# Decode attention and mixer on one core: loads by half chunks at the layer changes, and a sixth kept V chunk

## The chip, the cores and the metric

The kernel runs on one core of a Trainium2 chip. The metric is the device time of one execution in microseconds (us); the median of the runs is compared. In the profile PE is TensorE, DVE is VectorE, ACT is ScalarE, POOL is GpSimd and SP is the engine whose queue issues nearly all transfers here. The core has 16 DMA engines, and every transfer of this kernel is spread over all of them.

## What is computed

Two tokens (a batch of 2, one position each, 512 channels) pass through two layers. A layer is an attention block followed by a small mixer, each with a residual:

```
x = x + attention(layernorm(x), k_cache, v_cache, wq, wo)
x = x + mixer(layernorm(x), w1, b1, w2, b2)      # layernorm, one 1 x 1792 product, gelu, 1792 x 1
x = x + attention(layernorm(x), k_cache, v_cache, wq, wo)
x = x + mixer(layernorm(x), w1, b1, w2, b2)
```

The attention has 32 query heads on 8 heads of keys and values, with 32768 cached keys of 128 channels for each of the 2 x 8 pairs of token and head. All is float32. Both layers use the same caches and weights. K and V of one pair are 16.8 MB each, so one layer reads 537 MB and two layers 1074 MB, less what stays on the chip between them.

## The kernel before, in words

**Units and chunks.** A unit is (layer, token b, head h), and there are 32 of them, numbered n in an order of their own. K and V of a unit are cut into 8 chunks c of 4096 keys. One chunk fills 16 KB in each of the 128 partitions and weighs 2.1 MB ("2048 KB" in the profile). For a K chunk PE runs 8 products (line 359, shown as 16 matmul records, because each float32 product leaves two), for a V chunk 8 more (line 492). In most of the run, chunks are loaded four at a time in one transfer of 8 MB.

**Memory.** The tile `mem` holds 14 numbered cells of one chunk each (the last one shorter). Cells 0 to 8 are the ring for passing chunks, cells 9 to 12 hold the weights of the heads that pass, and cell 13 is a rest of 10 KB per partition. Around the changes of layer the cells 3 to 9, 11 and 13 are needed for what stays, and the passing chunks have cells 0, 1 and 2 alone: this is `limit=RING` with `RING` 3, and there each transfer is one chunk.

**What stays.** Head 7 is the keeper. Its units of layer 0 and layer 1 for the same token follow one another closely (units 13 and 15 for token 0, units 16 and 18 for token 1), so that what was loaded for layer 0 is read again for layer 1 without a second load. `KEPT_K` lists three K chunks (2, 4, 5 in cells 9, 7, 8); `KEPT` lists the V chunks with the number of quads (eighths of a chunk) and the cell: 1, 3, 5, 6, 7 whole, and of chunk 4 five quads. Two more quads of chunk 4 are set aside in PSUM (`IN_PSUM`).

**The two changes of layer.** Unit 13 is (0, 0, 7) and ends layer 0 for token 0; its mixer must be done before the layer-1 unit 15 = (1, 0, 7) can form its query. Between them unit 14 = (0, 1, 5) is worked on, and the mixer's steps are spread between its K chunks (lines 714 and 190). The same happens for token 1 with units 16 = (0, 1, 7), 17 = (1, 0, 5) and 18 = (1, 1, 7). Unit 19 is (1, 1, 5), and unit 20 = (1, 0, 0) is the first of layer 1 on a passing head, whose weights (2.1 MB of Wq and Wo) are loaded into cell 9 during unit 19's K chunks.

**The order of work.** The order is written out by a planner: `parts` gives the pieces in which a unit's K and V are loaded, `stream` sorts them, and `at(time, ...)` hangs the small steps to slots of that order (one slot is one chunk). The last loop walks through `stream`: it issues a load, then the products of that piece, then the steps due. PE executes this order. SP executes the loads in the same order, one after another, and runs ahead as far as memory allows: a load whose place is still being read waits on PE's semaphore, and every load behind it waits as well.

**Places.** `buffer` (line 126) takes the place in the ring that was touched longest ago. `load_k` and `load_v` (lines 336 and 424) issue the transfers at lines 344, 433 (a kept part) and 446. `load_weights` issues at line 115.

Of the kernel before, what the change touches and what calls it, by code (L numbers as in the profile page):

```python
# [13 lines left out]
P = 128  # L14
CK = 4096
JT = CK // P
NG = 4
SUB = 2
PACK = 4
GROUPS = ((0, 4), (4, 4))  # L20
RING = 3
# [1 line left out]


KEPT_K = {2: 9, 4: 7, 5: 8}
KEPT = {1: (8, 6), 3: (8, 11), 4: (5, 13), 5: (8, 3), 6: (8, 4), 7: (8, 5)}
REST = 5
IN_PSUM = (4, 5, 2)
ASIDE = 3
# [3 lines left out]
PIECES = (32, 16, 8, 4, 4)  # L33
THIN = 16
QT = 4
# [7 lines left out]
def gqa_mixer_kernel(ctx: ExitStack, tc: tile.TileContext, x, kt, v, wqo, cols, out):  # L43
# [17 lines left out]
    nc = tc.nc  # L61
    B, D = out.shape
    U = kt.shape[0]
    DH = D // NG
    NCH = kt.shape[1] // (CK * DH)
    HKV = U // B
# [31 lines left out]
    WCELL0, WCELLS = RING * RING, 4  # L98
# [3 lines left out]
    mem = const.tile([P, (WCELL0 + WCELLS) * CK + REST * QT * DH], F32, name="mem")  # L102

    def cells(k, m=1):
        return mem[:, k * CK : (k + m) * CK]
# [9 lines left out]
        nc.sync.dma_start(cells(cell), wqo[h])  # L115


    used = [0] * (WCELL0 + WCELLS + 1)
    clock = [0]

    def touch(k, m=1):
        clock[0] += 1
        for j in range(k, k + m):
            used[j] = clock[0]

    def buffer(m, limit):

        k = min(range(0, limit - m + 1, m if limit % m == 0 else RING), key=lambda k: max(used[k : k + m]))
        touch(k, m)
        return cells(k, m)  # L130

    load_weights(0, WCELL0)
    cols_sb = sm["cols"]
# [35 lines left out]
    kept = [pfix.tile([P, 512], F32, name=f"kept{k}") for k in range(IN_PSUM[2])]  # L169
# [29 lines left out]
    def first_input():  # L199

        t = spot()
        cen, sq = (t[:, k * B * DT : (k + 1) * B * DT].rearrange("p (b d) -> p b d", b=B) for k in range(2))
        m, rs = (t[:, (2 * DT + k) * B : (2 * DT + k + 1) * B] for k in range(2))
        p = misc()
        nc.tensor.matmul(p[:, : B * DT], ones, xcols.rearrange("p b d -> p (b d)"), start=True, stop=True)
        nc.vector.tensor_reduce(m, p[:, : B * DT].rearrange("p (b d) -> p b d", b=B), axis=AX.X, op=ALU.add)
        nc.vector.tensor_scalar_mul(m, m, 1.0 / D)
        for b in range(B):
            nc.vector.tensor_scalar_sub(cen[:, b, :], xcols[:, b, :], m[:, b : b + 1])
        nc.vector.tensor_mul(sq, cen, cen)  # L210
# [107 lines left out]
    BESIDE = N3 + 1, 5  # L318
# [11 lines left out]
    def piece(a, u, c, m):  # L330

        c0, size = next(g for g in GROUPS if g[0] <= c < sum(g))
        rows = a[u, c0 * CK * DH : (c0 + size) * CK * DH].rearrange("(p f) -> p f", p=P)
        return rows[:, (c - c0) * CK : (c - c0 + m) * CK]

    def load_k(n, c, m, limit):
        layer, b, h = unit_of(n)
        stay = h == keeper and c in KEPT_K
        own = KEPT_K[c] if stay else KEPT[1][1] if (n, c) == BESIDE else None
        if own is not None:  # L340
            touch(own, m)
        t = buffer(m, limit) if own is None else cells(own, m)
        if not (stay and layer):
            nc.sync.dma_start(t, piece(kt, b * HKV + h, c, m))
        for j in range(m):
            k_at[n, c + j] = t[:, j * CK : (j + 1) * CK]

    def k_chunk(n, c):

        kc = k_at.pop((n, c))  # L350
        half, i = divmod(c, PACK)
        if i == 0:
            sc_ps[n, half] = pscore.tile([P, 512], F32, name="scores")
        w = CK // (NG * SUB)
        for k in range(SUB):
            at = R * (SUB * i + k)
            q = qpad[n % 2][:, 28 - at : 60 - at]
            for g in range(NG):
                nc.tensor.matmul(  # L359
                    sc_ps[n, half][32 * g : 32 * g + 32, :],  # L360
                    q,
                    kc[:, (k * NG + g) * w : (k * NG + g + 1) * w],
                    start=(i == 0 and k == 0),
                    stop=(i == PACK - 1 and k == SUB - 1),
                )
        if i == PACK - 1:
            if half == 0:
                mx[n] = field(n, 0, HALVES)
            nc.vector.tensor_reduce(mx[n][:, half : half + 1], sc_ps[n, half], axis=AX.X, op=ALU.max)  # L369
# [49 lines left out]
    def stays(n, c):  # L419

        quads, cell = KEPT.get(c, (0, 0)) if unit_of(n)[2] == keeper else (0, 0)
        return quads, mem[:, cell * CK : cell * CK + quads * QT * DH]

    def load_v(n, c, m, limit):
        layer, b, h = unit_of(n)
        src = piece(v, b * HKV + h, c, m)
        stay, own = stays(n, c)
        if stay:
            touch(KEPT[c][1])
        w = QT * DH  # L430
        f = stay * w
        if stay and layer == 0:
            nc.sync.dma_start(own, src[:, :f])
        if stay == JT // QT:
            return
        t = buffer(m, limit)
        banks = []
        if stay and (c, stay) == IN_PSUM[:2]:
            banks = [(k, t[:, f + i * w : f + (i + 1) * w]) for i, k in enumerate(kept)]
        if layer:  # L440
            for k, quad in banks:
                nc.vector.tensor_copy(quad, k)
                f += w
        last = n == NU - 1 and c + m == NCH
        for k in PIECES if last else (m * JT - f // DH,):
            nc.sync.dma_start(t[:, f : f + k * DH], src[:, f : f + k * DH])
            f += k * DH
        if not layer:
            for k, quad in banks:
                nc.vector.tensor_copy(k, quad)  # L450
        for j in range(m):
            v_at[n, c + j] = t[:, j * CK : (j + 1) * CK]

    last_sums = {}

# [21 lines left out]
        nc.vector.tensor_mul(oT[n][:, :, 1], po[:, :R], rl[n])  # L477

    def v_chunk(n, c):
        w = QT * DH  # L480
        very_last = n == NU - 1 and c == NCH - 1
        stay, own = stays(n, c)
        vc = v_at.pop((n, c), None)
        half, i = divmod(c, PACK)


        a, c2 = divmod(i, PACK // 2)
        quads = JT // QT - (THIN // QT if very_last else 0)
        for q in range(quads):
            g = q % NG  # L490
            col = (c2 * (JT // QT) + q) * 32 + a * R * QT
            nc.tensor.matmul(  # L492
                acc[32 * g : 32 * g + R * QT, :],
                S[half][:, col : col + R * QT],
                (own if q < stay else vc)[:, q * w : (q + 1) * w],
                start=(c == 0 and q < NG),
                stop=(c == NCH - 1 and q >= quads - NG),
            )
        if very_last:
            add_tiles()  # L500

        for j in range(quads * QT, JT):
            q, t = divmod(j, QT)
            g = j % NG
            col = (c2 * (JT // QT) + q) * 32 + a * R * QT + t * R
            nc.tensor.matmul(
                kept[0][32 * g : 32 * g + R, :DH],
                S[half][:, col : col + R],
                vc[:, j * DH : (j + 1) * DH],
                start=(j < quads * QT + NG),  # L510
                stop=True,
                skip_group_check=True,
            )
# [107 lines left out]
    def last_mixer(n):  # L621
# [2 lines left out]
        layer, b, h = unit_of(n)  # L624
        w = D // 2
        st, mv, rs = ln_st.rearrange("p (k s) -> p k s", k=2), ln_mv, ln_rs
        space = buffer(2, 2 * RING)
        tiles = [space[:, k * D : (k + 1) * D] for k in range(JT2)]
        flat = tiles[JT2 - 1]
        y = row_tile()  # L630
# [152 lines left out]
    for n in range(NU):  # L783
# [55 lines left out]
        if units[n] == lay[layer, b][-1]:  # L839
# [30 lines left out]
            if layer + 1 < LAYERS:  # L870
                at(e + 2, to_columns, key)
                mixed[key] = e + 2

    first_input()
    for step in range(3):
        make_q(0, step)
# [4 lines left out]

    t = 0
    for _, is_v, n, c, m, limit in stream:
        if not is_v and (n, c) in SOONER:
            load_v(*SOONER[n, c], m, limit)
        if not is_v or (n, c) not in SOONER.values():
            (load_v if is_v else load_k)(n, c, m, limit)
        for j in range(m):
            (v_chunk if is_v else k_chunk)(n, c + j)
            t += 1  # L890
            run(t)
# [58 lines left out]
```

## Time and profile before

| | |
|---|---|
| median of 3 runs | 2502.08 us (2501.8 to 2502.96) |
| span of the profiled execution | 2500.0 us (the median of the runs lies 2.1 us above it) |
| PE busy | 1383.1 us, 55% of the span |
| DVE, ACT busy | 222.4 us and 185.4 us |
| moved by DMA | 1067.23 MB, mean 427 GB/s |
| read from HBM | 1065.91 MB |
| transfers of one chunk of K, of V | 44 and 35, 2048 KB each |
| transfers of four chunks | 48 of K and 47 of V |

The page shows in its first part how long each engine was busy, and in its second part the span in 40 slices with the busy tenths of each engine, the granted clock of PE and the DMA's rate. Its third part shows the DMA queues; q1 is SP's. The chain of waits goes back from the last instruction to what released it at each step. A timeline row has its start, its length, the engine, the line, the operation, the tiles and the number of records, and in brackets how long the engine stood idle before it and what ended that. On the chain a piece named DMA begins with the issue of the transfer and ends when the engine that waited for it could start.

### The profile page before, as it was taken

Reading aid. Unit: us, or ns where it says so; the run is one execution under the profiler, and the core shown is the slowest. Engines: PE = TensorE matmul, PEld = TensorE weight load, DVE = VectorE, ACT = ScalarE, POOL = GpSimd, SP = SyncE. Lnnn points to the kernel's source line nnn. Section 1 sums busy time; section 2 is a strip of 40 time slices with the busy share of each in tenths; the row PEclk is TensorE's granted clock in tenths of the full one; section 3 lists DMA queues with packets and bytes.
Section 4 is the critical chain, followed back from the end, with each engine's and each line's share of the span. In section 5 each row is a group of like instructions: output and inputs, shape, how many; then the busy total and the mean of one; then the engine's idle time right before and its main releaser. Section 6 shows DMA issues by size and latency. Waiting matters only on the chain.

```text
span 2500.0 us, 20528 instructions
## 1 busy us (share of the span) xinstructions
PE 1383.1 (55%) x9326; PEld 375.5 (15%) x9326; DVE 222.4 (9%) x610; ACT 185.4 (7%) x550; POOL 4.9 (0%) x17
## 2 busy tenths in 40 slices
PE   4545554645445554657667775455546454455546
PEld 1111111111111111111111211111111111111112
DVE  0000000000000000001111110000000000010002
ACT  0000000000000000001012010000000000011002
POOL 0000000000000000000000000000000000000000
PEclk8777777877777777879888977677778777777778
DMA  9999999999999999999999999999999999999996
GB/s 419 436 433 430 433 435 430 436 430 430 433 433 431 434 429 435 425 423 421 426 427 427 423 430 430 432 435 434 432 430 435 435 423 435 433 433 426 432 429 292
DMA packets 31200, 1067.23 MB, mean 427 GB/s; under 512 B 3717, under 2 KB 3721, under 8 KB 4618
## 3 DMA queue, kind: packets, MB, share of 16 engines
q1 hardware_dynamic: 30824, 1065.89, 99.2%
q8 instruction: 73, 1.20, 0.2%
q14 instruction: 13, 0.11, 0.0%
q10 hardware_dynamic: 290, 0.04, 0.0%
HBM read 1065.91 MB, written 0.00 MB: 426 GB/s over the span
## 4 chain that ended last, share of the span: by engine, by line
DMA 74%; PE 24%; issue 0%; DVE 0%; ACT 0%; SPq 0%; POOL 0%; ACTq 0%
DMA mem<-in_v_dram 65%; PE acc L492 19%; DMA mem<-in_kt_dram 9%; PE scores L359 3%; PE bcast L292 1%; PE rows L190 0%; PE small L385 0%; PE small L521 0%; ACT S L714 0%; PE kept L671 0%; PE small L379 0%; PE small L256 0%; ACT mem L681 0%; ACT mem L693 0%; PE bcast L575 0%
## 5 line engine op out<-in xcount | busy, mean ns | idle before, releaser
L359 PE MATMUL scores<-mem,small_sb 128*32 128x512 f32 x4096 | 620.6, 722 | 592.0 <-DMA mem<-in_kt_dram 591.6
L492 PE MATMUL acc<-mem,S 128*16 128x512 f32 x4088 | 614.1, 738 | 468.2 <-DMA mem<-in_v_dram 462.5
L359 PEld LDWEIGHTS scores<-mem,small_sb 128*32 128x32 f32 x4096 | 151.1, 127 | 970.5 <-issue 895.5
L396 ACT ACTIVATE S<-S,small_sb 128x128 f32<-128x128 f32 x240 | 123.5, 519 | 2102.4 <-DVE small_sb L387 1636.6
L492 PEld LDWEIGHTS acc<-mem,S 128*16 128x16 f32 x4088 | 134.8, 110 | 831.7 <-issue 693.2
L369 DVE TENSOR_REDUCE small_sb<-scores 128x1 f32<-128x512 f32 x64 | 44.2, 691 | 874.1 <-PE scores L359 874.1
L391 DVE STREAM_TRANSPOSE S<-scores 128x512 f32<-128x512 f32 x64 | 45.4, 710 | 131.4 <-PE acc L492 131.4
L292 PE MATMUL kept<-mem,small_sb 128*2 128x512 f32 x104 | 50.9, 615 | 1.7 <-DVE small_sb L218 1.7
L190 PE MATMUL rows<-mem,small_sb 128*1 128x512 f32 (+1 forms) x276 | 48.4, 603 | 3.1 <-ACT mem L714 2.4
L396 ACT ACTIVATION_READ_ACCUMULATOR S<-S,small_sb 128x1 f32 x240 | 44.8, 187 | 0.0
L381 DVE TENSOR_REDUCE small_sb<-small 1x4 f32<-1x128 f32 x32 | 8.8, 276 | 280.7 <-PE small L379 280.7
L460 DVE SCALAR_TENSOR_TENSOR S<-acc,small_sb,S 128x128 f32<-128x128 f32 x93 | 32.6, 351 | 3.3
L523 DVE RECIPROCAL small_sb<-small 128x4 f32<-128x4 f32 x32 | 5.9, 185 | 292.1 <-PE small L521 292.1
L531 DVE TENSOR_TENSOR small_sb<-small,small_sb 128x4 f32<-128x4 f32 x31 | 5.1, 164 | 278.2 <-PE small L529 278.2
L714 ACT ACTIVATE S<-bcast,small_sb 128x512 f32<-128x512 f32 x28 | 20.7, 775 | 96.1 <-DVE small_sb L583 82.6
L190 PE MATMUL rows<-S,small_sb 128*1 128x512 f32 (+1 forms) x56 | 21.2, 591 | 8.1 <-ACT S L714 8.1
L304 PE MATMUL small<-small_sb,mem 2*128 2x2 f32 x112 | 15.1, 252 | 17.9 <-DVE mem L301 17.9
L458 DVE TENSOR_SCALAR S<-acc,small_sb 128x128 f32<-128x128 f32 x31 | 10.8, 350 | 128.8 <-PE acc L492 128.8
L292 PE MATMUL bcast<-mem,small_sb 128*1 128x512 f32 (+1 forms) x40 | 19.1, 609 | 1.2 <-DVE small_sb L261 1.2
L529 PEld LDWEIGHTS small<-small_sb,S 128*128 128x128 f32 x62 | 11.6, 234 | 48.8 <-issue 36.0
L304 PEld LDWEIGHTS small<-small_sb,mem 2*128 2x128 f32 x112 | 13.9, 190 | 30.5 <-DVE mem L301 27.3
L529 PE MATMUL small<-small_sb,S 128*128 128x4 f32 x62 | 14.3, 301 | 4.9 <-DVE S L460 4.9
(132 smaller groups left out, 267.7 us busy)
## 6 DMA issues: line engine op xcount, KB each, us to landing
mem<-in_kt_dram SPq DMA_DIRECT2D x44, 2048.0 KB, 12.7
mem<-in_v_dram SPq DMA_DIRECT2D x35, 2048.0 KB, 13.9
mem<-in_v_dram SPq DMA_DIRECT2D x9, 4096.0 KB, 32.7
mem<-in_wqo_dram SPq DMA_DIRECT2D x14, 2048.0 KB, 33.8
mem<-in_kt_dram SPq DMA_DIRECT2D x7, 4096.0 KB, 25.7
mem<-in_v_dram SPq DMA_DIRECT2D x2, 1280.0 KB, 13.6
mem<-in_v_dram SPq DMA_DIRECT2D x2, 768.0 KB, 18.6
mem<-in_v_dram SPq DMA_DIRECT2D x4, 256.0 KB, 28.8
```

The lines of the kernel that those rows point to most:

```text
L190: nc.tensor.matmul(rows[32 * g : 32 * g + b + 1, :], weights if b else weights[:, 1:], row, start=False, stop=True, skip_group_check=True,)
L292: nc.tensor.matmul(q_ps[n][:m, :], xnT[:, d, b : b + m], wq_at(h)[:, d, :], start=(d == 0), stop=(d == DT - 1),)
L304: nc.tensor.matmul(pt[:, r * m : (r + 1) * m], q_row[n][:m, r * DH : (r + 1) * DH], ident[:m, :m], start=True, stop=True,)
L359: nc.tensor.matmul(sc_ps[n, half][32 * g : 32 * g + 32, :], q, kc[:, (k * NG + g) * w : (k * NG + g + 1) * w], start=(i == 0 and k == 0), ...
L369: nc.vector.tensor_reduce(mx[n][:, half : half + 1], sc_ps[n, half], axis=AX.X, op=ALU.max)
L391: nc.vector.transpose(S[half], sc_ps[n, half])
L396: nc.scalar.activation(s[:, :, h], s[:, :, h], AF.Exp, bias=neg[n][:, h : h + 1], scale=SCALE, accum_out=lsum[n][:, half, h : h + 1],)
L458: nc.vector.tensor_scalar_mul(t, acc[:, :DH], mask[:, 0:1])
L460: nc.vector.scalar_tensor_tensor(t, acc[:, k * DH : (k + 1) * DH], mask[:, k : k + 1], t, op0=ALU.mult, op1=ALU.add)
L492: nc.tensor.matmul(acc[32 * g : 32 * g + R * QT, :], S[half][:, col : col + R * QT], (own if q < stay else vc)[:, q * w : (q + 1) * w], st ...
L529: nc.tensor.matmul(po[:, :R], asb, selh, start=True, stop=True)
L714: nc.scalar.activation(hid[key, f], px[key], AF.Gelu_apprx_tanh, bias=shift[key][:, f : f + 1], scale=slope[key][:, f : f + 1],)
```

## The change

The loads at `limit == RING` no longer take the oldest of three whole cells. The bookkeeping in slots (`busy`, `now`, `booked`, `closed`) says until when each half cell is read, when a cell is booked for something that stays, and when it closes. `spread` looks for a whole cell among 0 to 9 that has been idle for two slots and stays clear until the chunk is done; if there is one, the chunk is loaded whole as before. If there is none, the chunk is loaded as two transfers of half a chunk, 8 KB per partition, each into the half cell that is free first. The products now read their quads from a list (`quads`), so that the two halves need not lie side by side; their number and order stay. `KEPT` gains chunk 2, all 8 quads, in cell 2, which leaves cells 0 and 1, four halves, in the tightest stretch.

```diff
-KEPT = {1: (8, 6), 3: (8, 11), 4: (5, 13), 5: (8, 3), 6: (8, 4), 7: (8, 5)}
+KEPT = {1: (8, 6), 2: (8, 2), 3: (8, 11), 4: (5, 13), 5: (8, 3), 6: (8, 4), 7: (8, 5)}
...
-    def buffer(m, limit):
-
-        k = min(range(0, limit - m + 1, m if limit % m == 0 else RING), key=lambda k: max(used[k : k + m]))
-        touch(k, m)
+    def buffer(m, limit, until):
+
+        k = min(range(0, limit - m + 1, m), key=lambda k: idle(k, m))
+        assert idle(k, m) <= now[0]
+        hold(k, m, until)
         return cells(k, m)
+
+    def half(until):
+
+        k = min((j for j in range(2 * NCH) if clear(j // 2, until)), key=lambda j: busy[j])
+        assert busy[k] <= now[0]
+        busy[k] = until
+        return mem[:, k * HB : (k + 1) * HB]
+
+    def clear(k, until):
+
+        return until <= closed.get(k, until) and all(r <= now[0] or r >= until + 1.5 for r in booked.get(k, ()))
+
+    def spread(until):
+
+        whole = [k for k in range(WCELL0 + 1) if idle(k) <= now[0] - 2 and clear(k, until)]
+        if whole:
+            k = min(whole, key=idle)
+            hold(k, 1, until)
+            return [cells(k)]
+        return [half(until - 0.5), half(until)]
...
-        t = buffer(m, limit) if own is None else cells(own, m)
-        if not (stay and layer):
-            nc.sync.dma_start(t, piece(kt, b * HKV + h, c, m))
+        until = k_done[n, c + m - 1]
...
+        elif limit == RING:
+            bufs = spread(until)
+        else:
+            bufs = [buffer(m, limit, until)]
+        src, f = piece(kt, b * HKV + h, c, m), 0
+        for t in bufs:
+            if not (stay and layer):
+                nc.sync.dma_start(t, src[:, f : f + t.shape[-1]])
+            f += t.shape[-1]
...
-                    kc[:, (k * NG + g) * w : (k * NG + g + 1) * w],
+                    kc[k * NG + g],
...
+    for n in (N1, N2):
+        for c in KEPT_K:
+            booked.setdefault(KEPT_K[c], []).append(k_done[n, c] - 1)
+        for c in KEPT:
+            first = next((k_done[k] - 1 for k, e in SOONER.items() if e == (n, c)), v_done[n, c] - 1)
+            booked.setdefault(KEPT[c][1], []).append(first)
+    booked[KEPT[1][1]].append(k_done[BESIDE] - 1)
+    closed[WCELL0], closed[WCELL0 - 1] = kbeg[N3 + 2] - 10, kbeg[N3 + 2] - 8
```

`load_v` is changed in the same way; the part of chunk 4 that doesn't stay goes into one half cell.

In the changed program the order of the products, of the steps on DVE and ACT, and of the chunks that are loaded stays as it was. SP's transfers of `mem` are these: at each of the two changes 11 chunks (K chunks 4 to 7 and V chunks 0 to 4 of unit 14, and K chunks 0 and 1 of unit 15; units 17 and 18 at the second change) come as 22 halves into cells 0 and 1, all others as whole chunks; V chunk 2 of units 15 and 18 isn't loaded. Later V chunk 6 of unit 14 and K chunk 7 of unit 15 go to cell 9, some chunks to cells 7 and 8. K chunk 3 of unit 19 goes to cell 9, and the next transfer in SP's order is the weights of unit 20's head, into cell 9 as well. Before, that K chunk went to cell 1.

More of the change, by code (lines that the diff above doesn't have):

```diff
@@ L115, in load_weights, with hold, idle, quads @@
         nc.sync.dma_start(cells(cell), wqo[h])
[L118 to L124, printed above, removed]
-    def buffer(m, limit):
-        k = min(range(0, limit - m + 1, m if limit % m == 0 else RING), key=lambda k: max(used[k : k + m]))
-        touch(k, m)
-        return cells(k, m)
+    HB = CK // 2
+    busy = [0] * 2 * (WCELL0 + WCELLS + 1)
+    now = [0]
+    def hold(k, m, until):
+        for j in range(2 * k, 2 * (k + m)):
+            busy[j] = max(busy[j], until - 0.5 * (m == 1 and j == 2 * k))
+    def idle(k, m=1):
+        return max(busy[2 * k : 2 * (k + m)])
+    def buffer(m, limit, until):
+        k = min(range(0, limit - m + 1, m), key=lambda k: idle(k, m))
+        assert idle(k, m) <= now[0]
+        hold(k, m, until)
+        return cells(k, m)
+    def half(until):
[12 more added lines that the diff above has]
+        return [half(until - 0.5), half(until)]
+    def quads(a):
+        w = QT * P
+        return [a[:, i : i + w] for i in range(0, a.shape[-1], w)]
+    booked, closed = {}, {}
     load_weights(0, WCELL0)
@@ L339, in load_k @@
         own = KEPT_K[c] if stay else KEPT[1][1] if (n, c) == BESIDE else None
+        until = k_done[n, c + m - 1]
         if own is not None:
-            touch(own, m)
-        t = buffer(m, limit) if own is None else cells(own, m)
-        if not (stay and layer):
-            nc.sync.dma_start(t, piece(kt, b * HKV + h, c, m))
+            if stay and not layer:
+                until = k_done[units.index((1, b, h)), c + m - 1]
+            hold(own, m, until)
+            bufs = [cells(own, m)]
+        elif limit == RING:
[7 more added lines that the diff above has]
+            f += t.shape[-1]
+        at = [q for t in bufs for q in quads(t)]
         for j in range(m):
-            k_at[n, c + j] = t[:, j * CK : (j + 1) * CK]
+            k_at[n, c + j] = at[j * (JT // QT) : (j + 1) * (JT // QT)]
     def k_chunk(n, c):
@@ L353, in k_chunk @@
             sc_ps[n, half] = pscore.tile([P, 512], F32, name="scores")
-        w = CK // (NG * SUB)
         for k in range(SUB):
@@ L427, in load_v @@
         stay, own = stays(n, c)
-        if stay:
-            touch(KEPT[c][1])
+        until = v_done[n, c + m - 1]
         w = QT * DH
         f = stay * w
[L432 to L439, printed above, removed]
+        at = quads(own) if stay else []
+        if stay:
+            if layer == 0:
+                nc.sync.dma_start(own, src[:, :f])
+                hold(KEPT[c][1], 1, v_done[units.index((1, b, h)), c])
+            if stay == JT // QT:
+                v_at[n, c] = at
+                return
+            bufs = [half(until)[:, : CK - f]]
+        elif limit == RING:
+            bufs = spread(until)
+        else:
+            bufs = [buffer(m, limit, until)]
+        rest = [q for t in bufs for q in quads(t)]
+        banks = list(zip(kept, rest)) if stay else []
         if layer:
@@ L442, in load_v @@
                 nc.vector.tensor_copy(quad, k)
-                f += w
         last = n == NU - 1 and c + m == NCH
-        for k in PIECES if last else (m * JT - f // DH,):
-            nc.sync.dma_start(t[:, f : f + k * DH], src[:, f : f + k * DH])
-            f += k * DH
+        for t in bufs:
+            if layer and stay:
+                f += len(banks) * w
+                t = t[:, len(banks) * w :]
+            for k in [k * DH for k in PIECES] if last else (t.shape[-1],):
+                nc.sync.dma_start(t[:, :k], src[:, f : f + k])
+                f, t = f + k, t[:, k:]
         if not layer:
@@ L450, in load_v @@
                 nc.vector.tensor_copy(k, quad)
+        at = at + rest
         for j in range(m):
-            v_at[n, c + j] = t[:, j * CK : (j + 1) * CK]
+            v_at[n, c + j] = at[j * (JT // QT) : (j + 1) * (JT // QT)]
     last_sums = {}
@@ L479, in v_chunk @@
     def v_chunk(n, c):
-        w = QT * DH
         very_last = n == NU - 1 and c == NCH - 1
-        stay, own = stays(n, c)
-        vc = v_at.pop((n, c), None)
+        vc = v_at.pop((n, c))
         half, i = divmod(c, PACK)
@@ L494, in v_chunk @@
                 S[half][:, col : col + R * QT],
-                (own if q < stay else vc)[:, q * w : (q + 1) * w],
+                vc[q],
                 start=(c == 0 and q < NG),
@@ L508, in v_chunk @@
                 S[half][:, col : col + R],
-                vc[:, j * DH : (j + 1) * DH],
+                vc[q][:, t * DH : (t + 1) * DH],
                 start=(j < quads * QT + NG),
@@ L626, in last_mixer @@
         st, mv, rs = ln_st.rearrange("p (k s) -> p k s", k=2), ln_mv, ln_rs
-        space = buffer(2, 2 * RING)
+        space = buffer(2, 2 * RING, now[0])
         tiles = [space[:, k * D : (k + 1) * D] for k in range(JT2)]
@@ L883, in gqa_mixer_kernel @@
     for _, is_v, n, c, m, limit in stream:
+        now[0] = t
         if not is_v and (n, c) in SOONER:
```

## The prediction

> **What bounds the kernel now.** I read the page first: busy times, the 40 slices, the queues and the chain of waits.
>
> ```profile
> span 2500.0 us, 20528 instructions
> ...
> PE 1383.1 (55%) x9326; PEld 375.5 (15%) x9326; DVE 222.4 (9%) x610; ACT 185.4 (7%) x550; POOL 4.9 (0%) x17
> ...
> DMA  9999999999999999999999999999999999999996
> GB/s 419 436 433 430 433 435 430 436 430 430 433 433 431 434 429 435 425 423 421 426 427 427 423 430 430 432 435 434 432 430 435 435 423 435 433 433 426 432 429 292
> ...
> q1 hardware_dynamic: 30824, 1065.89, 99.2%
> ...
> DMA 74%; PE 24%; issue 0%; DVE 0%; ACT 0%; SPq 0%; POOL 0%; ACTq 0%
> ```
>
> DMA is at 9 tenths or more in 39 slices of 40, and SP's queue alone fills 99.2% of 16 engines' span. PE is busy little more than half the time. So the time is bytes over rate, and every other engine matters only where it frees a place too late for the next load. The slices from 1000 to 1440 us (the two changes) read 421 to 427 GB/s, those next to them 429 to 435. To see whether that dip is idle time, I asked for four stretches: with 8 MB loads (first and last row) and with 2 MB loads (the middle two). The last three columns are PE's clock, the DMA share and GB/s.
>
> ```profile
> core 0: us, PE busy (x) PEld busy (x) DVE busy (x) ACT busy (x) POOL busy (x), PEclk, DMA share, GB/s
> 600.00:950.00 350.00, 180.66 (x1230) 49.91 (x1225) 25.86 (x75) 19.35 (x72) 0.00 (x0) 0.75 1.00 432
> 1130.00:1300.00 170.00, 117.38 (x754) 30.10 (x754) 25.12 (x60) 17.04 (x33) 1.09 (x2) 0.87 1.00 424
> 1350.00:1470.00 120.00, 83.12 (x524) 21.36 (x522) 16.96 (x39) 15.81 (x32) 0.55 (x1) 0.88 1.01 426
> 1600.00:2000.00 400.00, 208.18 (x1400) 57.65 (x1404) 27.62 (x80) 19.35 (x72) 0.00 (x0) 0.75 1.00 433
> ```
>
> The DMA share is 1.00 in all four. The changes are not starved; their shorter rows only move less per unit of busy time. There is no stall for this change to remove. It can win by bytes alone, and lose by shorter rows and by new waits in SP's queue.
>
> **The change, part by part.** All times are made against the profiled execution (span 2500.0 us); the median of the runs is 2502.08, so 2.1 us are added at the end.
>
> *Bytes saved.* V chunk 2 is not loaded again in units 15 and 18: two loads of 2.097 MB. At 425 GB/s (the middle of the 2 MB rows) one takes 4.93 us, two **-9.9 us**. No other load goes away, so this is certain as long as the queue stays full.
>
> *Shorter rows.* A 2 MB load is 128 rows of 16 KB; in an 8 MB load the same bytes are 32 rows of 64 KB. By the rows above, 2.097 MB take 4.93 us at 425 and 4.84 at 433, so 96 more rows cost 0.09 us. A chunk cut in two has 128 more rows: 0.12 us. There are 22 such chunks: **+2.7 us**. From below it is nothing, from above twice that, 5.3.
>
> *What a wait costs when the queue has run empty.* The trace of before has this once, at the start, on the chain of waits:
>
> ```profile
> 0.74 0.39 SPq L115
> 1.19 0.41 SPq L344
> 1.64 45.70 DMA mem<-in_kt_dram
> ```
>
> From the first issue at 0.74 to the moment at 47.34 when PE could use the third transfer, 18.87 MB were moved (one of 2.10, two of 8.39), 43.6 us at 433 GB/s. The other **3.0 us** lie between issue and first byte and between last byte and PE's start. In a full queue they are hidden. Where a load waits for PE to read the very last chunk that is in flight, they show, and PE's reading with them. The Trainium skill (DMA: Bandwidth & Descriptors, "Anatomy of one DMA — SWDGE (gpsimd) path") gives about 2.0 us as the fixed part of one DMA on another issue path; by it each empty-queue wait below would be up to 1.0 us shorter, and the sum would come to -0.9 or 2501.2 us. The start of this trace shows 3.0.
>
> *The first halves.* K chunk 4 now comes as a half into the place of chunk 2's first half, where it had a third cell. What is queued ahead of it is chunk 3 alone. At the first change the timeline has:
>
> ```profile
> 1143.29 3.47 PE L492 MATMUL acc<-mem,S 128*16 128x512 f32 x16 [1.90 <-DMA mem<-in_v_dram]
> ...
> 1149.88 3.20 PE L359 MATMUL scores<-mem,small_sb 128*32 128x512 f32 x16
> ...
> 1154.41 1.92 PE L359 MATMUL scores<-mem,small_sb 128*32 128x512 f32 x16
> ```
>
> The last V chunk has landed at 1143.29 (PE waited for it). K chunks 2 and 3 follow at 4.93 each, so chunk 3 lands at 1153.15. Between, PE turns the finished sums into rows, and so begins chunk 2 only at 1149.88; its first half is free at the middle, 1151.5. With an empty queue the new half lands at 1151.5 + 3.0 + 2.5 = 1157.0; in a full one it would at 1153.15 + 2.5 = 1155.6. Lost: 1.4 us. At the second change:
>
> ```profile
> 1341.93 3.38 PE L359 MATMUL scores<-mem,small_sb 128*32 128x512 f32 x16
> ...
> 1346.46 1.92 PE L359 MATMUL scores<-mem,small_sb 128*32 128x512 f32 x16
> ```
>
> Chunk 3 is read from 1346.46 on, as it lands; half of chunk 2 is free at 1343.6, and 3.0 more is 1346.6: 0.1 us lost. Together **+1.5 us**, from nothing to 4.5 (1.4 at both, and the 1.7 of half a slow chunk once).
>
> *The weights behind a K chunk.* SP now issues K chunk 3 of unit 19 into cell 9 and directly behind it the weights into the same cell. They wait until PE has read that chunk; the remaining K chunks of unit 19 stand behind them on SP, which issues in order, so DMA runs empty. Before, the timeline shows:
>
> ```profile
> 1444.67 0.42 SPq L115 DMA_DIRECT2D mem<-in_wqo_dram  x1
> ...
> 1452.78 1.91 PE L492 MATMUL acc<-mem,S 128*16 128x512 f32 x16
> ...
> 1455.47 1.92 PE L359 MATMUL scores<-mem,small_sb 128*32 128x512 f32 x16 [0.78 <-DMA mem<-in_kt_dram]
> ```
>
> The weights were issued at 1444.67, well before PE began K chunk 3 at 1455.47, and PE stood waiting for that chunk (0.78 us). So PE will be ready; it reads for 1.92 us and then 3.0 us pass: **+4.9 us**. From below it is 1.9: the 16 engines need not end together, and those that are last lose less. From above it is 6.5, with a read at the low clock (3.47 us in the row at 1143.29). Later nobody lacks the weights or these chunks: the whole stream only moves back.
>
> *Four halves instead of three wholes.* Before, two other loads (9.9 us) lie between a chunk's landing and the load that takes its place, which needs 3.0 + 1.92 = 4.9: 5.0 to spare. Now three halves, 7.5 us with their extra rows, stand against 3.0 and half a reading, 1.0 (1.7 at the low clock): 2.8 to 3.5 to spare. PE's hold-ups in the mixer are to be set against that:
>
> ```profile
> 1172.83 1.98 PE L359 MATMUL scores<-mem,small_sb 128*32 128x512 f32 x16
> ...
> 1178.64 1.91 PE L492 MATMUL acc<-mem,S 128*16 128x512 f32 x16 [1.64 <-ACT S L411]
> 1180.48 1.13 PE L726 MATMUL bcast<-S,small_sb 128*128 128x512 f32 x2
> 1182.62 1.91 PE L492 MATMUL acc<-mem,S 128*16 128x512 f32 x16 [1.01 <-DMA mem<-in_v_dram]
> ...
> 1188.68 0.62 PE L492 MATMUL acc<-mem,S 128*16 128x512 f32 x3
> ```
>
> The starts of four chunks are 5.8, 4.0 and 6.1 us apart, against 5.1 that DMA needs for one in halves. One is at most 1.0 late, less than the spare, and between them PE waits for data again. So most hold-ups hide; where PE's clock drops in the same place, some show. I take 1.0 us at each change, **+2.0 us**, with nothing as the one end and 4.0 at each change as the other (the spare used up, and one slow reading more).
>
> *Costed at nothing.* Products, DVE and ACT steps stand in the old order with the old shapes. SP issues 20 transfers more, at 0.4 us each by the rows of the start, beside loads of 2.5 us. Loads outside the changes have their old places or their old distance.
>
> Sum: -9.9 + 2.7 + 4.9 + 1.5 + 2.0 = **+1.2 us**, a span of 2501.2, and on the median **2503.3 us**.
>
> **The rivals.**
>
> *The saving comes through.* The drained queue costs little, because the 16 engines end apart and the last ones restart at once. Then the weights cost the lower end, 1.9, the other waits nothing: -9.9 + 2.7 + 1.9 = -5.3, or 2496.8 us. For it speaks the DMA share of 1.01 in one stretch (packets overlap a little); against it, that all 16 engines need the same issue from SP.
>
> *The ring of four halves runs dry in the mixer.* It decides from the point where PE falls more than 2.8 us behind, which two hold-ups of 1.0 and a drop to the low clock (1.6 more for a chunk, 3.47 against 1.91) would reach. Then both changes lose the upper end, 4.0 each: +1.2 - 2.0 + 8.0 = +7.2, or 2509.3 us, slower than before. For it speaks that PE's hold-ups come one after another; against it, that PE's row at 1182.62 still ends a wait for data.
>
> *Each transfer pays its fixed part.* The same fit of the Trainium skill, read as a serial cost, would add 20 x 2.0 = 40 us. In rows: the 2 MB stretches show 0.09 us more per 2.1 MB than the 8 MB ones, so it can't be more than hundredths here; the price with 0.09 for each of 20 transfers is 1.8 us, inside my 2.7. By the page's figure the time would be 2541 us.
>
> *The bytes are not saved.* The change then gives 2503.3 + 9.9 = 2513.2 us. The list of transfers excludes it.
>
> **How the numbers follow.** My forecast (2503.3 us; of its own 2498 to 2507) has 0.62, the saving come through 0.15, the dry ring 0.20, the fixed part 0.02 and the unsaved bytes 0.01. The range reaches down to the first rival and up to the second: 2497 to 2509 us. It leaves out the sum of all lower ends and that of all upper ends, which would have to come together. A measurement of this kernel can tell about 0.2% (5 us) from no change: faster by more than that is the first rival (0.15), within it the forecast (0.62), slower the others (0.23).
>
> **What would show it.** HBM read falls by 4.2 MB to 1061.7 MB. SP's row of the weights (line 115) comes directly after a K chunk's last product near 1450 us, and the 20 us around it fall to some 75% of the usual GB/s. At the first halves, near 1152 us, a smaller dip; elsewhere in the two changes 415 to 420 GB/s. If that dip is missing, the first rival holds; if rates stay low between 1155 and 1200 us, the second. I would be wrong altogether if a load outside the changes had become late.

## The result

The changed kernel takes 2507.74 us (median; 2505.08 to 2511.08), the kernel before 2502.22 (2501.31 to 2504.93). The ratio is 1.0022, with a 95% interval of 1.0015 to 1.0029: 3.8 to 7.3 us slower, where the prediction had 1.2. The profiled execution took 2506.53 us, with a span of 2504.7. Two executions that took far longer are left out of every ratio, range and median: one of e5 below (2778.07 us) and one of the kernel before beside it (4043.92).

The page of the changed kernel, with the lines that answer to those quoted of before:

```profile
span 2504.7 us, 20561 instructions
...
GB/s 419 434 433 432 435 433 429 434 433 436 433 431 431 435 430 430 429 425 406 415 426 398 408 389 431 436 433 431 431 433 434 434 435 432 430 433 435 430 432 287
...
q1 hardware_dynamic: 33704, 1061.70, 98.8%
...
DMA 74%; PE 25%; issue 0%; DVE 0%; ACT 0%; SPq 0%; POOL 0%; ACTq 0%; DVEq 0%
```

SP's queue moved 4.19 MB less (1065.89 before), so the bytes are saved. DMA still makes up 74% of the chain of waits, as before. Outside the changes the slices are as before; in slices 19 and 20 (406, 415) and 22 to 24 (398, 408, 389) they aren't, where before read 421 to 430.

To turn that into time a full queue with the same short rows is needed for comparison. One experiment gives it: the kernel before with the 22 chunks cut in two and no new wait (e4, below). Its stretches, and then those of the changed kernel (stretch; its length, PE's busy time; PE's clock, DMA share, GB/s):

```profile
1140.00:1170.00 30.00, 23.58 (x150) 0.92 1.00 420
1170.00:1200.00 30.00, 22.77 (x132) 0.93 1.02 422
1200.00:1220.00 20.00, 13.89 (x82) 0.76 1.01 422
1340.00:1370.00 30.00, 23.79 (x138) 0.94 1.01 420
1370.00:1400.00 30.00, 22.15 (x128) 0.90 1.02 423
1400.00:1420.00 20.00, 14.25 (x92) 0.84 1.01 424
1440.00:1480.00 40.00, 25.40 (x164) 0.72 1.01 426
```

```profile
1140.00:1170.00 30.00, 22.92 (x148) 0.95 0.95 388
1170.00:1200.00 30.00, 22.11 (x132) 0.96 1.01 414
1200.00:1220.00 20.00, 13.08 (x74) 0.73 0.99 395
1340.00:1370.00 30.00, 22.70 (x136) 1.00 0.93 371
1370.00:1400.00 30.00, 20.43 (x128) 0.94 1.00 403
1400.00:1420.00 20.00, 13.83 (x84) 0.91 0.98 393
1440.00:1480.00 40.00, 22.29 (x158) 0.79 0.87 361
```

Length times (1 - GB/s over GB/s of e4) is the time that DMA lost: 2.3, 0.6 and 1.3 us in the first change, 3.5, 1.4 and 1.5 in the second, 6.1 around the weights, together 16.6 us. A single stretch is good to about 1 us: without any halves, the kernel before reads 411 in the first row and e2 (below) 407 in the second. The 4.19 MB saved are worth 9.9 us at 425 GB/s, an estimate; the losses are more than that, and they lie in three kinds of places.

**The weights.** The timeline of the changed kernel, PE's rows and SP's (the bracket is idle time before and what ended it):

```profile
1459.83 1.92 PE L401 MATMUL scores<-mem,small_sb 128*32 128x512 f32 x16 [0.79 <-DMA mem<-in_kt_dram]
1461.57 1.90 PE L542 MATMUL acc<-mem,S 128*16 128x512 f32 x16
1474.58 3.22 PE L401 MATMUL scores<-mem,small_sb 128*32 128x512 f32 x16 [11.11 <-DMA mem<-in_kt_dram]
```

```profile
1461.81 0.33 SPq L115 DMA_DIRECT2D mem<-in_wqo_dram  x1
1462.19 0.91 SPq L385 DMA_DIRECT2D mem<-in_kt_dram  x2
```

PE was ready and waited 0.79 us for K chunk 3, read it for 1.92, and only then SP issued the weights (1461.81), with the next K chunks behind them. PE then stood for 11.11 us. How full DMA was meanwhile:

```profile
1455.00:1458.00 3.00, 3.00 (x27) 1.00 0.75 317
1458.00:1461.00 3.00, 2.21 (x24) 1.00 0.03 11
1461.00:1464.00 3.00, 2.47 (x24) 1.00 0.54 104
1464.00:1467.00 3.00, 0.00 (x0) 1.00 0.94 393
```

The first row is the one that the forecast lacks. Before 1458, while PE still waited for chunk 3, DMA moved 317 GB/s: some of the 16 engines had done their part of the chunk and had nothing more. GB/s is the measure here, not the share: from 1461 to 1464 the share is already 0.54 while only 104 GB/s move.

**The first halves.** The same at the start of the changes. PE's and SP's rows of the first one, then three stretches of the first change and two of the second:

```profile
1148.49 1.90 PE L401 MATMUL scores<-mem,small_sb 128*32 128x512 f32 x16
...
1149.59 13.62 SPq L385 DMA_DIRECT2D mem<-in_kt_dram  x7
...
1153.17 1.92 PE L401 MATMUL scores<-mem,small_sb 128*32 128x512 f32 x16 [1.73 <-DMA mem<-in_kt_dram]
```

```profile
1146.00:1149.00 3.00, 1.75 (x18) 1.00 0.68 289
1149.00:1152.00 3.00, 2.44 (x18) 1.00 0.75 276
1148.50:1150.50 2.00, 2.00 (x21) 1.00 0.50 213
1341.00:1343.00 2.00, 1.75 (x20) 1.00 0.45 188
1343.00:1345.00 2.00, 2.00 (x14) 1.00 0.54 143
```

SP issued the first half at 1149.59, 3.6 us before PE could begin chunk 3, so by the last landing it was in time. Yet DMA had fallen to 289 GB/s from 1146 on, and between 1148.5 and 1150.5 its share is 0.50: only half of the 16 engines were at work.

**The ends of the changes.** V chunk 5 of unit 14 takes a whole cell again:

```profile
1201.37 5.32 SPq L497 DMA_DIRECT2D mem<-in_v_dram  x2
...
1211.26 0.33 SPq L385 DMA_DIRECT2D mem<-in_kt_dram  x1
```

```profile
1204.37 1.94 PE L401 MATMUL scores<-mem,small_sb 128*32 128x512 f32 x8 [0.55 <-DMA mem<-in_kt_dram]
...
1209.34 1.85 PE L542 MATMUL acc<-mem,S 128*16 128x512 f32 x8 [0.48 <-DMA mem<-in_v_dram]
...
1221.33 3.54 PE L401 MATMUL scores<-mem,small_sb 128*32 128x512 f32 x16 [5.19 <-DMA mem<-in_kt_dram]
```

Its cell holds both halves of unit 15's K chunk 1. The load is the second in the first SP row, issued as PE's reading that began at 1204.37 ends; between that second half's landing and this load only one chunk in halves lies in the queue, 5.0 us. The next load, K chunk 3 of unit 15 (issued at 1211.26), waits for V chunk 4's second half in the same way (PE's reading from 1209.34), with V chunk 5 alone as cover. Later PE waits 5.19 us for it.

### The profile page after: what moved, and what is told of

Its sections match the earlier page's. It is cut to its first block, busy times and chain, and to the rows that moved or that the text cites. A ratio compares the mean times of both kernels' runs of the same rounds, so it can differ in the third digit from the quotient of the medians.

```text
span 2504.7 us, 20561 instructions
## 1 busy us (share of the span) xinstructions
PE 1384.2 (55%) x9326; PEld 374.2 (15%) x9326; DVE 222.7 (9%) x610; ACT 185.4 (7%) x550; POOL 4.9 (0%) x17
## 4 chain that ended last, share of the span: by engine, by line
DMA 74%; PE 25%; issue 0%; DVE 0%; ACT 0%; SPq 0%; POOL 0%; ACTq 0%; DVEq 0%
DMA mem<-in_v_dram 38%; DMA mem<-in_kt_dram 36%; PE scores L401 11%; PE acc L542 11%; PE rows L222 1%; PE kept L324 1%; PE bcast L324 0%; PE small L579 0%; PE small L427 0%; ACT S L764 0%; PE small L571 0%; PE kept L721 0%; PE small L421 0%; PE bcast L601 0%; PE small L288 0%
## 5 line engine op out<-in xcount | busy, mean ns | idle before, releaser
L421 PE MATMUL small<-small_sb 128*1 128x128 f32 x64 | 17.0, 360 | 0.6 <-DVE small_sb L417 0.6
```

The costliest lines, as they stand in the source:

```text
L421: nc.tensor.matmul(pm[:1, :P], mxa, ident, start=True, stop=True)
```

## The experiments

Two theories stood against each other. **A**: the queue that runs dry in these places took the gain. **B**: the halves themselves are dear, and a wait costs little. All times are medians, of 15 executions for the changed kernel, 4 for e3 and 11 for the others; each ratio is against the kernel before on the same chip. The experiments ran on several chips, on which the kernel before took 2501.6 to 2502.1 us; where that bears on two experiments, what they differ by when each is first taken against the kernel before on its chip stands beside their difference, as "corrected for the chip". None of these kernels leaves work out.

| kernel | us (range) | ratio, 95% interval |
|---|---|---|
| changed kernel | 2507.74 (2505.08 to 2511.08) | 1.0022 (1.0015 to 1.0029) |
| e1_weights_free | 2501.01 (2498.78 to 2504.84) | 0.9997 (0.9988 to 1.0005) |
| e2_no_sixth | 2501.93 (2501.42 to 2504.33) | 1.0000 (0.9991 to 1.0009) |
| e3_no_halves | 2521.03 (2516.72 to 2522.89) | 1.0072 (1.0056 to 1.0087) |
| e4_rows_only | 2503.01 (2502.81 to 2504.72) | 1.0003 (0.9995 to 1.0012) |
| e6_wider_halves | 2500.14 (2497.25 to 2506.90) | 0.9996 (0.9987 to 1.0005) |
| e7_five_halves | 2499.61 (2498.79 to 2501.56) | 0.9990 (0.9981 to 0.9998) |
| e8_first_halves | 2499.00 (2496.72 to 2503.45) | 0.9991 (0.9982 to 1.0000) |
| e9_five_all | 2499.93 (2499.61 to 2502.78) | 0.9994 (0.9986 to 1.0003) |
| e5_five_old_end | 2501.75 (2499.10 to 2502.97) | 0.9999 (0.9990 to 1.0007) |
| e10_five_weights | 2504.97 (2504.23 to 2506.86) | 1.0012 (1.0004 to 1.0021) |

### The weights wait taken away

```diff
-    closed[WCELL0], closed[WCELL0 - 1] = kbeg[N3 + 2] - 10, kbeg[N3 + 2] - 8
+    closed[WCELL0], closed[WCELL0 - 1] = kbeg[N3 + 2] - 11, kbeg[N3 + 2] - 8
```

> The changed kernel, but K chunk 3 of unit 19 goes to a cell that the weights do not use, so that no load stands behind its reading. All halves stay. Theory A (the queue that runs dry in three places took the gain: weights some 6 us, first halves and the ring of halves some 7 us together, shorter rows 2.3 us): 2507.7 - 6 = about 2501.7 us (2500.7 to 2503), GB/s near 1450 us back at the usual value. Theory B (the halves themselves are dear, some 0.5 us for each of the 22 chunks, and a wait costs little because the 16 engines end apart): the weights cost at most 1.9 us, so 2505.8 us.

Measured 2501.01 us, 6.7 less than the changed kernel, and the stretch of the weights is full again (e1):

```profile
1440.00:1480.00 40.00, 27.35 (x186) 0.84 1.01 427
```

That is theory A, and far from B's 2505.8.

### No sixth chunk, the new bookkeeping alone

```diff
-KEPT = {1: (8, 6), 2: (8, 2), 3: (8, 11), 4: (5, 13), 5: (8, 3), 6: (8, 4), 7: (8, 5)}
+KEPT = {1: (8, 6), 3: (8, 11), 4: (5, 13), 5: (8, 3), 6: (8, 4), 7: (8, 5)}
```

> The changed kernel without the sixth kept V chunk; with that no half chunks arise, all loads of the changes are whole ones in three cells, placed by the new bookkeeping. Theories A and B both give the kernel before, 2502.2 us within 0.5. If it differs by more, a part of the 5.5 us comes from other places for loads and belongs to neither.

Measured 2501.93 us, as expected: other places by themselves cost nothing that shows.

### The sixth chunk with two whole cells

```diff
-        return [half(until - 0.5), half(until)]
+        k = min((k for k in range(NCH) if clear(k, until)), key=idle)
+        hold(k, 1, until)
+        return [cells(k)]
```

> The changed kernel with the sixth chunk kept, but the tight stretches go by two whole cells and no halves. A load then waits for the reading of the chunk before the last one: one load (4.9 us) covers a reading and a restart (4.9 us by the rows of before). Theory A: no spare, every hold-up of PE in the two changes reaches DMA: 22 chunks with 0.5 to 1.5 us each in place of the halves' 9 us, 2510 to 2532 us. Theory B: the halves' 0.5 us per chunk goes away and a wait costs little: 2497 to 2503 us.

Measured 2521.03 us, 13.3 more than with halves, inside A's range and far above B's. In e3 DMA moves less all through the second change:

```profile
1340.00:1370.00 30.00, 18.99 (x121) 1.00 1.00 392
1370.00:1400.00 30.00, 21.34 (x120) 0.94 0.87 329
1400.00:1420.00 20.00, 14.81 (x70) 0.57 0.91 356
```

### The shorter rows alone

In the kernel before:

```diff
-            nc.sync.dma_start(t, piece(kt, b * HKV + h, c, m))
+            src = piece(kt, b * HKV + h, c, m)
+            step = CK // 2 if limit == RING and (n, c) in SPLIT_K else m * CK
+            for i in range(0, m * CK, step):
+                nc.sync.dma_start(t[:, i : i + step], src[:, i : i + step])
...
-        for k in PIECES if last else (m * JT - f // DH,):
+        for k in PIECES if last else (JT // 2, JT // 2) if limit == RING and (n, c) in SPLIT_V else (m * JT - f // DH,):
```

> The kernel before with the same 22 chunks issued as two transfers each into their old whole cells; no sixth chunk, no new waits. Theory A: the shorter rows alone, 22 x 0.10 = 2.3 us, so 2504.5 us (2503.5 to 2505.5). Theory B: 0.5 us for each, 2502.2 + 11 = 2513 us.

Measured 2503.01 us, 1.0 more than before (from 1.2 less to 3.0 more by the interval): even less than A's 2503.5 to 2505.5, and B falls. By the median, 22 transfers more in a full queue come to 0.05 us each; the interval doesn't exclude nothing. The Trainium skill's fixed part of about 2.0 us for one DMA (DMA: Bandwidth & Descriptors, "Anatomy of one DMA — SWDGE (gpsimd) path"), given for another issue path, doesn't show as a serial cost on this queue.

### The ends of the changes by halves

On e1:

```diff
-        whole = [k for k in range(WCELL0 + 1) if idle(k) <= now[0] - 2 and clear(k, until)]
+        whole = [k for k in range(WCELL0 + 1) if idle(k) <= now[0] - (2 if k > 1 else 4) and clear(k, until)]
```

> The kernel e1_weights_free, and at the end of each change six more half loads: V chunk 5 (and 7) and the next unit's K chunk 0 still go by halves, where the changed kernel took a whole cell again and so waited for both halves' readers. Theory A (these two loads stand in the queue alone: in e1's trace the landings there come 2.0 us late at each change): 2501.0 - 4.0 + 0.5 for shorter rows = 2497.5 us (2496 to 2499.5), GB/s of 1200 to 1220 us and of 1400 to 1420 us back above 410. Rival C (PE's hold-ups set the pace in the changes, so the wait only moves to the next load): 2500 to 2501.5 us, with the dip some 10 us later.

(The K chunk in question is chunk 3 of units 15 and 18, not chunk 0.) Measured 2500.14 us, outside A's range (2496 to 2499.5) and just inside C's (2500 to 2501.5), with executions from 2497.25 to 2506.90, so that the median alone doesn't decide. The profiled one was the slowest. In it the ends are full again or nearly so (the rows at 1200 and 1400; e1 had 385 and 390), so the wait did not move on to the next load, as rival C has it. But the beginnings were worse than in e1 (384 at 1140, 403 at 1340); the rows of e6:

```profile
1140.00:1170.00 30.00, 21.97 (x128) 0.89 0.89 350
1200.00:1220.00 20.00, 14.08 (x74) 0.66 1.01 411
1340.00:1370.00 30.00, 22.35 (x129) 0.91 0.95 373
1400.00:1420.00 20.00, 16.35 (x106) 0.92 1.02 424
```

Why, its timeline shows at the second change. PE comes to K chunk 2 at 1344.89 and reads it in 3.37 us; in the changed kernel's profile that began at 1342.11 and took 1.90.

```profile
1344.89 3.37 PE L401 MATMUL scores<-mem,small_sb 128*32 128x512 f32 x16
```

```profile
1342.11 1.90 PE L401 MATMUL scores<-mem,small_sb 128*32 128x512 f32 x16
```

The granted clock during this reading is 0.54 in e6 and 1.00 in the changed kernel. PE's pace there differs from one profile to the next, and the first half of chunk 4 has to wait for it. So A and C each hold a part, as these profiles have it: cover decides how much of PE's lateness reaches DMA.

### Five halves, half of the sixth chunk kept

On e6 (with the place's bookings by halves):

```diff
-KEPT = {1: (8, 6), 2: (8, 2), 3: (8, 11), 4: (5, 13), 5: (8, 3), 6: (8, 4), 7: (8, 5)}
+KEPT = {1: (8, 6), 2: (4, 2), 3: (8, 11), 4: (5, 13), 5: (8, 3), 6: (8, 4), 7: (8, 5)}
...
-        k = min((j for j in range(2 * NCH) if clear(j // 2, until)), key=lambda j: busy[j])
+        k = min((j for j in range(2 * NCH) if clear(j // 2, until) or j == 5), key=lambda j: busy[j])
```

> The kernel e6_wider_halves, but of the sixth chunk only a half is kept, so that the tight stretch has five halves and a load waits for the reading of the one five before it; half of the saved bytes is given up (+4.9 us). Theory A (what is left of the loss sits in the first halves, some 3 us in both changes, and in the ring of four, some 2.5 us): most of it goes, 2497.5 + 4.9 - 4 = 2498.5 us (2497 to 2500). Rival C (the loss is PE's pace, whatever the number of halves): 2497.5 + 4.9 = 2502.5 us and more.

Measured 2499.61 us, inside A's 2497 to 2500, and C's 2502.5 falls. The executions lie within 2.8 us of each other, where e6's lie within 9.7. Half of the saved bytes is gone (4.9 us), and nothing is lost by it: the waits were worth as much. Of e7:

```profile
1140.00:1170.00 30.00, 24.21 (x150) 0.91 0.98 401
1200.00:1220.00 20.00, 14.46 (x86) 0.74 1.01 416
1340.00:1370.00 30.00, 23.68 (x138) 0.94 1.00 416
1400.00:1420.00 20.00, 13.88 (x88) 0.79 1.02 427
```

This is the one kernel whose interval lies wholly below 1: 2.4 us faster than the kernel before.

### K chunks 2 and 3 in two transfers, with four halves and with five

On e6, and the same on e7:

```diff
             bufs = spread(until)
+            if n in (N1 + 1, N2 + 1) and c in (2, 3):
+                bufs = [bufs[0][:, :HB], bufs[0][:, HB:]]
```

> The kernel e6_wider_halves, and K chunks 2 and 3 of units 14 and 17 are loaded as two transfers each into their old cells, so that PE can read the first half of chunk 2 before the whole has landed, and three halves instead of two stand behind it. Theory A: at the second change PE waits for chunk 2 to land, so the first halves' wait (1.2 to 2.3 us in the traces) goes; at the first change PE is late by its own work on rows and nothing is won; 0.3 for rows: 2497.5 - 1.2 = about 2496.3 us (2495 to 2497.5). Rival C (PE is late by its own work at both): 2497.8 us.

Measured 2499.00 us, 1.1 less than e6. A has 1.2 less, C 0.3 more, but e8's executions lie 6.7 us apart, so this doesn't decide. In its profile what A names isn't seen: the dip at the second change is still there (e8), and PE read chunk 2 in 3.55 us, at a granted clock of 0.50:

```profile
1340.00:1370.00 30.00, 23.84 (x138) 0.94 0.95 371
```

```profile
1340.32 3.55 PE L403 MATMUL scores<-mem,small_sb 128*32 128x512 f32 x16
```

> The kernel e7_five_halves, and K chunks 2 and 3 of units 14 and 17 as two transfers each into their old cells. Now every load of the changes has at least 9.8 us of other loads between the landing that PE needs and itself. Theory A (what costs time is cover below some 8 us): the last wait of e7 (1.2 us at the first halves of the first change) shrinks to half or less, 0.3 us for rows, so 2499.6 - 0.6 + 0.3 = 2499.3 us (2498.3 to 2500.3). Rival C (PE's own work on rows makes it late there whatever the cover): 2499.9 us.

Measured 2499.93 us, where the expectations were 2499.3 and 2499.9: too close together to tell. Against e8 it loads 4.9 us more and is 0.9 slower (1.4 corrected for the chip), so a fifth half is worth some 4 us.

### The two other waits, one at a time, on e7

e5 has e7's diff without e6's line; e10 is e7 with `kbeg[N3 + 2] - 10` back.

> The kernel e7_five_halves, but the ends of the changes as in the changed kernel: V chunk 5 and the next unit's K chunk 0 take whole cells again and wait for both halves' readers, with one load (5.0 us) as cover. Five halves hold the other waits at nothing, so that this one is seen by itself. Theory A: 2.0 us at each change (e1's landings), 0.5 less for rows: 2499.6 + 3.5 = 2503.1 us (2501.6 to 2504.6), narrower in its runs than e6. Rival C (with the slack of five halves the queue is ahead, and the wait hides): 2499.1 us.

Measured 2501.75 us, 2.1 more than e7 (2.6 corrected for the chip), between A (3.5) and C (-0.5), and inside A's range at its lower end (2501.6). In e5's profile the first change lost at its end, the second hardly:

```profile
1200.00:1220.00 20.00, 12.28 (x78) 0.76 0.95 385
1400.00:1420.00 20.00, 13.88 (x90) 0.84 1.00 411
```

> The kernel e7_five_halves, but K chunk 3 of unit 19 goes to cell 9 again and the weights wait behind its reading, as in the changed kernel, and nothing else in the changes waits long. Theory A (16 engines empty from their mean end to the restart, 6.2 us in the changed kernel's landings): 2499.6 + 6.2 = 2505.8 us (2505 to 2506.8). The step as forecast (read 1.92 and restart 3.0, counted from the last landing): 2499.6 + 4.9 = 2504.5 us. Rival (only the last engines lose): 2501.5 us.

Measured 2504.97 us, 5.4 more than e7 (5.8 corrected for the chip): between the last landing's 4.9 and the mean's 6.2. The rates of its stretch give 6.0:

```profile
1440.00:1480.00 40.00, 22.93 (x144) 0.70 0.87 362
```

So the runs put the weights at 5.4 to 6.7 us, around the 6.1 that the rates give; the rival in which only the last engines lose (1.9) is out. The difference between 4.9 and 6.2 the medians alone don't settle.

## Why the prediction was right and wrong

The list of mechanisms lacked one, the ends of the changes. The weights and the first halves were priced too low, the shorter rows too high. The price by the rates is in the third column, the price by the runs in the last.

| step | forecast, us | by the rates | by the runs |
|---|---|---|---|
| bytes saved | -9.9 | 4.19 MB fewer | not taken alone |
| shorter rows | +2.7 (0 to 5.3) | | +1.0 (e4) |
| weights behind a K chunk | +4.9 (1.9 to 6.5) | 6.1 | 6.7 (e1), 5.4 to 5.8 (e10) |
| first halves | +1.5 (0 to 4.5) | 2.3 + 3.5 - 0.6 = 5.2 | with the next row some 4 (e8, e9) |
| four halves, in the mixer | +2.0 (0 to 8) | 0.6 + 1.4 = 2.0 | |
| ends of the changes | nothing | 1.3 + 1.5 = 2.8 | 2.1 to 2.6 (e5) |
| sum | +1.2 | +7.2 with e4's rows | +5.5 |

(The 0.6 is what the kernel before lost itself in its row 1140 to 1170, at 411 GB/s against e4's 420. The prediction found no stall there, because its stretch ran from 1130 to 1300; of the four DMA shares that it read as 1.00 one is 1.01.) The rates give 1.7 us more than the medians, within the interval of 3.8 to 7.3; they are of one execution, and leave out what the rest of the span did in it. In the two profiles the spans differ by 4.7 us only: before has 423 and 426 GB/s in its slices 33 and 37, where the changed kernel has 435, which makes some 3 us.

**The step that failed** is the first halves, in the sentence "half of chunk 2 is free at 1343.6, and 3.0 more is 1346.6: 0.1 us lost". Its times came true: SP's first half went out at 1343.21, and PE began chunk 3 at 1346.02. At the first change the half was even free 1.9 us earlier than forecast (1149.59 against 1151.5), so that by the forecast's own count nothing was lost there. But the loss was counted from the last landing, as if the queue were full up to there. The 16 engines end apart. In the changed kernel's trace the 16 landing events of K chunk 3 at the first change run from 1147.2 to 1153.1 us, 1150.3 in the mean: eight of them by 1148.8, the other eight from 1151.7 on.

PE waits for the last landing, while the first engine is without work from 1147.2 on, and every idle microsecond of an engine counts a sixteenth. What counts is the time from each engine's own end to the restart. At the first change nearly all of that loss is the first eight's. Where all have ended before the restart, as at the weights, it is the time from the mean landing: from K chunk 3's last landing (1459.79) to that of the weights (1469.54) are 9.75 us, 4.8 more than the 4.93 of a load, but from the mean of the one (1458.08) to the mean of the other (1469.16) are 11.08 us, 6.2 more. In a full queue the skew costs nothing that shows: the stretch from 1143 to 1146, where it was already there, has a DMA share of 1.01 and 431 GB/s. The stretches at 289, 276, 188 and 143 GB/s, all before PE could begin chunk 3, show the loss. The weights' step has the same flaw, and its lower bound ("those that are last lose less") took the skew as a gain: the last engines lose no more, but the others do.

**The step that was missing** is the end of the changes. "Loads outside the changes have their old places or their old distance" overlooked the seam between halves and wholes. A whole load that takes a cell with two halves in it waits for the second one's reader, and has one chunk as cover (5.0 us) where the steady halves have three halves (7.5).

**What held.** The bytes came through, and DMA stayed the bound. Near the weights, the 20 us from 1455 on fell to 296 GB/s of e4's 427, 69%, where some 75% had been named. The ring in the mixer lost, by the rates, the 2.0 us that it was given; two stretches that are good to about 1 us each make that agreement weak. The first rival (the saving comes through) fell with e1 and e10. The dry ring had the time nearly right (2509.3) with the wrong place: 8.0 us in the mixer, where it was 2.0 there and the rest mostly at both ends of the changes. The fixed part per transfer fell with e4. Outcome and range: 2507.74 lies inside 2497 to 2509, but outside the forecast's own 2498 to 2507, and on the side to which 0.23 was given, not on the one with 0.62. That the range held is partly luck: its upper end was set for a dry ring in the mixer, and other waits filled that room. The profiled execution was also a kind one: PE read chunk 2 at a granted clock of 1.00 at both changes, in 1.90 us, where the profile of before has 0.57 and 0.56, and 3.20 and 3.38 us.

What stays open: the first halves and the ring were not separated by runs, only by stretches of one execution. Of the 3.5 us at the second change 0.9 lie from 1350 to 1353 (300 GB/s), after PE had begun chunk 3, and may belong to the ring. And the part of the skew in the weights' price lies between 0.5 and 1.8 us (5.4 and 6.7 against 4.9).

## What to carry to other kernels

In a kernel that is bound by its load queue, list for every load what stands in the queue between the landing that its reader needs and itself, at the seams of a scheme above all, and price a place where that list is too short from each engine's own end, not from the last landing. Saved bytes are worth their rate only while that cover stays longer than the restart, the reading and PE's worst hold-up together: here a fifth half place was worth about as much as half of the saved chunk. A look at GB/s in stretches of a few microseconds, against a run with the same transfers and no waits, finds such losses to about 1 us, where PE's rows show a wait of another size (1.73 us at the first halves of the first change, against 2.3 by the rates).

## What the runs showed of the hardware

The 16 engines carry a skew through a full queue: 5.9 us between first and last landing of one 2 MB load before the first change, and 1.6 us for the first half after the queue had run dry there; at the weights 2.5 us before and 0.6 after.

How far the executions of one kernel scatter went with the places, though they run the same instructions: the kernels with four halves (changed kernel, e1, e6, e8) lie within 6.0 to 9.7 us, those with five (e5, e7, e9, e10) within 2.6 to 3.9, e3 with two whole cells within 6.2 (four executions), e2 and e4 with three whole cells within 2.9 and 1.9, and the kernel before within 2.4 to 3.9 on its chips. PE's reading of the same chunk, 1.90 us in one profile (granted clock 1.00) and 3.37 in another (0.54), is the likely source; no run holds the clock fixed, so that is not shown.
